# A fused attention, expert and MLP kernel: input conversion and transposition, token tiles and weight conversion in more stages, and one more GpSimd DRAIN

## Chip, core and metric

The kernel runs on one core of a Trainium2 chip. The metric is the device time of one execution in microseconds. Engines are named as in the profile: PE (TensorE matmul), PEld (its weight loads), DVE (VectorE), ACT (ScalarE), POOL (GpSimd), SP (SyncE, which here only issues DMAs). A "q" behind an engine's name is its sequencer.

## The reference

```python
scores_l = scale * np.matmul(q, k.transpose(0, 1, 3, 2))     # local window of 16, plus block summaries
a = softmax(concat(masked scores_l, scores_s + log(32)))
x = a @ concat(v, v_sum)                                     # (2, 8, 768, 64) -> 1536 tokens x 512
logits = x @ w_gate; noise_scale = log1p(exp(x @ w_noise))
top2 of (logits + noise_scale * noise), softmax weights
out[token] = sum over its 2 experts: weight * (relu(x @ w1[e]) @ w2[e])     # 8 experts, 512 -> 1024 -> 512
h = out @ w_in; g = relu(h) ** 2; result = g @ w_out         # 512 -> 2048 -> 512
```

All data are float32. Matrix products of the last two stages are made of three passes of a rounded float32 type: a high part times a high part, and two products with a low part, so each operand exists as a high tile (xh, wh, hh) and a low tile (xl, wl, hl).

## The kernel before

**Attention**, to about 140 us in the trace, is untouched by the change. It scatters every token's row into a table xg with one region for each expert.

**Units.** From then on the kernel is a loop over units g. Units 0 to 63 are eight experts (e = g // 8) of eight units each (f = g % 8); units 64 to 111 are three chunks of 512 tokens with 16 units each. In unit g PE does `h_unit(g)`, 12 matmuls into a PSUM tile ph, and then the second half of the unit before, `y_unit(g - 1)` or `o_part`, 12 matmuls into acc. Each engine and SP's queue run in the order in which the code emits their instructions; there is no scheduler in this part. The order within a unit is: the matmuls and what follows ph (ACT writes hh, DVE hl, at lines 771 and 772 for experts, 765 to 769 for chunks), `y_store` at an expert's first unit, the split of the weights three units ahead (`w_split`: ACT wh at line 186, DVE wl at line 190, then SP's load of the weights wr six units ahead into the buffer just freed), the steps of `plan`, the next expert's input, the table steps, and last `conv`.

**Next expert's input.** `x_load(e)` has SP read the region of expert e from xg into xin. `x_turn` first calls `x_flip` (DVE transposes of 32 x 32 blocks, xin to xtt, line 217), and then ACT writes xh (line 227). `x_rest` writes xl, on POOL when the source is xtt. The four column chunks c go to units f = 3, 4, 5, 6; under expert 0 two each to units 5 and 6. `x_load(e + 2)` comes behind chunk 3, `x_load(1)` at unit 2. `fill(e)`, at units 1, 4, 7 and so on to 19, has POOL write zeros into a part of xg by an indirect DMA; each x_load waits for all fills ahead of it in the program, and each fill for the x_loads ahead of it.

**Weight conversion.** The last stage's weights come as eight-byte words. `conv` turns 32 pieces (units in CG: 1, 3, 5, 7, 9, 12, ...): SP loads cr, `conv_bits` does four ACT instructions (lines 823 to 826) into the tiles c0, c1 and c2, `conv_end` two DVE instructions one unit later, and `conv_store` one unit after that stores c0 to w2f with a DMA on SP's queue. The pool cv gives each of these tiles two buffers, so the first ACT instruction of a piece (line 823) waits until the store of the piece before the last has landed.

**Token tiles.** Tiles t of 128 tokens pass through `gather` (POOL indirect DMAs from yg), `mix` (ACT line 1154, DVE line 1155, and a store to x2d on SP), `swap` (SP reads x2d back in another order) and `spread` (DVE transpose at line 1176 into z4, ACT xh at line 1182, DVE xl at line 1183). GT, GB, G0 and G1 say in which unit each step stands. Chunk 1 is first read in unit 80, chunk 2 in unit 96.

**End.** Four indirect DMAs on POOL write the last output tiles; a loop that runs zero times here follows (line 1308), then the closing barrier with a DRAIN of each engine (line 1363).

Of the kernel before, what the change touches and what calls it, by code (L numbers as in the profile page):

```python
# [22 lines left out]
DM = H * D  # L23
E = 8
# [109 lines left out]
def moe_pipeline_kernel(ctx: ExitStack, tc: tile.TileContext, qT, kT, vW, mk, idm, wg, noise, w1, w2, out):  # L134
# [85 lines left out]
    def x_turn(e, c, src=None):  # L220
        if c == 0:
            xh_t[e] = xp.tile([128, 4, 512], F32R, name="xh")
            xl_t[e] = xp.tile([128, 4, 512], F32R, name="xl")
        if src is None:
            x_flip(e, c)
            src = xt_t[e][:, c, 0:CAPS[e]]
        nc.scalar.activation(out=xh_t[e][:, c, 0:CAPS[e]], in_=src, func=AF.Copy)  # L227

    def x_rest(e, c, src=None):
# [585 lines left out]
    def conv_bits(i):  # L815
# [279 lines left out]
    def overflow():  # L1095
        n = nc.values_load(trips[0:1, 0:1], min_val=0, max_val=nck)
        with tc.For_i(0, n, 1):
# [11 lines left out]
            xt = yb.tile([128, DM], F32, name="x2")  # L1109
# [42 lines left out]
    def blend(ys, gates):  # L1152
        x2 = yb.tile([128, DM], F32, name="x2")
# [31 lines left out]
    def late_tokens():  # L1185
        n = nc.values_load(trips[0:1, 1:2], min_val=0, max_val=NT)
        with tc.For_i(0, n, 1):
# [9 lines left out]
            xt = yb.tile([128, DM], F32, name="x2")  # L1197
# [169 lines left out]
```

## Time and profile before

| | |
|---|---|
| median of 3 runs | 724.45 us (719.29 to 729.62) |
| profiled execution | 722.66 us, its span 720.9 us |
| mean granted clock of TensorE over the span | 0.956 |
| busy in the span: PE, DVE, ACT, POOL | 652.8, 431.9, 364.3, 134.6 us |
| expert and chunk stages on PE | 139.6 to 707.5 us |

A profiled execution is one run, and lies 1.8 us under the median. PE's busy time counts pipelined matmuls whose ends are modelled: two rows that follow each other without a pause overlap.

### The profile page before, as it was taken

To read this page: it belongs to the slowest core of one execution; us is meant where nothing else is said; L and a number is where in the kernel's file an instruction comes from. 1 tells how busy PE (TensorE), PEld (TensorE's weight loads), DVE (VectorE), ACT (ScalarE), POOL (GpSimd) and SP (SyncE) were. 2 spreads that over 40 slices of the span, in tenths; PEclk is the share of its full clock that TensorE was granted. 3 is DMA by queue.
4 is the path that set the end of the run, shared out by engine and by line. 5 is a ranking of instruction groups with operands and counts; after the bars stand their busy time and mean duration, and the time that the engine had idled before them with its cause. 6 is when DMAs were issued, how large, how long until landed. Compare 5 with 4: busy or idle time off the path is not lost.

```text
span 720.9 us, 11094 instructions
## 1 busy us (share of the span) xinstructions
PE 652.8 (91%) x3928; PEld 574.0 (80%) x3928; DVE 431.9 (60%) x952; ACT 364.3 (51%) x708; POOL 134.6 (19%) x199
## 2 busy tenths in 40 slices
PE   5787776998998899999999979999999999999992
PEld 4666554797998799899999878788888888888881
DVE  5757554585767676756575656666665565644530
ACT  3676351255563564667466656654454455434330
POOL 3000434313130111335113400310024100300002
PEclk9999776799999999999999999999999999999997
DMA  8877326279988777788878787865437555432101
GB/s 229 198 186 177 138 89 209 83 258 316 292 320 268 262 224 264 200 276 247 248 223 301 253 257 249 250 201 156 135 106 241 147 160 132 145 116 90 59 1 61
DMA packets 75739, 139.97 MB, mean 194 GB/s; under 512 B 9042, under 2 KB 44162, under 8 KB 74895
## 3 DMA queue, kind: packets, MB, share of 16 engines
q1 hardware_dynamic: 69566, 116.95, 55.4%
q0 software_dynamic: 6112, 22.25, 8.3%
q8 instruction: 33, 0.54, 0.3%
q14 instruction: 28, 0.22, 0.1%
HBM read 103.27 MB, written 34.88 MB: 192 GB/s over the span
## 4 chain that ended last, share of the span: by engine, by line
PE 31%; DMA 24%; issue 15%; ACT 11%; DVE 10%; SPq 4%; another core or an unknown queue 2%; POOL 1%; DVEq 0%; ACTq 0%; POOLq 0%
DMA w2f<-c 6%; DMA vB<-in_vW_dram 5%; PE ph L750 4%; PE ph L748 4%; PE ph L749 4%; DVE wl L190 4%; PE acc L748 4%; PE acc L749 4%; PE acc L750 4%; DMA wr<-in_w_dram 3%; ACT wh L186 3%; DMA yg<-ys 3%; DMA vB<-vm 2%; DMA xg<-z,tb_gi 2%
## 5 line engine op out<-in xcount | busy, mean ns | idle before, releaser
L750 PE MATMUL ph<-xl,wh 128*128 128x512 f32 (+8 forms) x448 | 163.0, 364 | 1.8 <-POOL xl L233 1.8
L748 PE MATMUL ph<-xh,wh 128*128 128x512 f32 (+8 forms) x448 | 162.9, 364 | 0.4 <-ACT xh L1182 0.4
L749 PE MATMUL ph<-xh,wl 128*128 128x512 f32 (+8 forms) x448 | 162.5, 363 | 0.0
L190 DVE TENSOR_TENSOR wl<-wr,wh 128x1024 fp32r<-128x1024 f32 x112 | 137.1, 1224 | 28.6 <-ACT wh L186 25.8
L186 ACT ACTIVATE wh<-wr 128x1024 fp32r<-128x1024 f32 x112 | 117.5, 1049 | 4.5 <-DMA wr<-in_w_dram 4.5
L748 PE MATMUL acc<-hh,wh 128*128 128x416 f32 (+7 forms) x256 | 89.4, 349 | 11.1 <-ACT hh L771 11.0
L750 PE MATMUL acc<-hl,wh 128*128 128x416 f32 (+7 forms) x256 | 90.2, 352 | 3.8 <-DVE hl L772 3.7
L750 PEld LDWEIGHTS ph<-xl,wh 128*128 128x128 f32 x448 | 84.2, 188 | 11.2 <-POOL xl L233 2.8
L748 PEld LDWEIGHTS ph<-xh,wh 128*128 128x128 f32 x448 | 84.3, 188 | 8.5 <-ACT xh L1182 0.8
L749 PEld LDWEIGHTS ph<-xh,wl 128*128 128x128 f32 x448 | 84.2, 188 | 7.6
L749 PE MATMUL acc<-hh,wl 128*128 128x416 f32 (+7 forms) x256 | 88.3, 345 | 0.0
L772 DVE SCALAR_TENSOR_TENSOR hl<-ph,hh 128x416 fp32r<-128x416 f32 (+7 forms) x64 | 36.5, 570 | 71.1 <-ACT hh L771 71.1
L748 PE MATMUL acc<-wh,hh 128*128 128x512 f32 x192 | 74.8, 389 | 0.6 <-DVE ys L797 0.6
L749 PE MATMUL acc<-wh,hl 128*128 128x512 f32 x192 | 74.8, 390 | 0.0
L750 PE MATMUL acc<-wl,hh 128*128 128x512 f32 x192 | 74.7, 389 | 0.0
L765 ACT ACTIVATE hr<-ph 128x512 f32<-128x512 f32 x48 | 28.7, 598 | 81.5 <-PE ph L750 81.5
L766 DVE SCALAR_TENSOR_TENSOR hg<-ph,hr 128x512 f32<-128x512 f32 x48 | 33.1, 691 | 60.5 <-ACT hr L765 56.9
L748 PEld LDWEIGHTS acc<-hh,wh 128*128 128x128 f32 x256 | 48.6, 190 | 14.5 <-ACT hh L771 14.3
L233 POOL TENSOR_TENSOR xl<-xtt,xh 128x424 fp32r<-128x424 f32 (+6 forms) x28 | 31.7, 1135 | 134.0 <-ACT xh L227 134.0
L750 PEld LDWEIGHTS acc<-hl,wh 128*128 128x128 f32 x256 | 48.7, 190 | 9.6 <-DVE hl L772 9.2
L769 DVE TENSOR_TENSOR hl<-hg,hh 128x512 fp32r<-128x512 f32 x48 | 33.3, 693 | 33.5 <-ACT hh L768 32.8
L768 ACT ACTIVATE hh<-hg 128x512 fp32r<-128x512 f32 x48 | 30.3, 632 | 39.2 <-DVE hg L766 39.2
(246 smaller groups left out, 934.7 us busy)
## 6 DMA issues: line engine op xcount, KB each, us to landing
wr<-in_w_dram SPq DMA_DIRECT2D x64, 512.0 KB
wr<-w2f SPq DMA_DIRECT2D x48, 512.0 KB
cr<-in_w_dram SPq DMA_DIRECT2D x32, 512.0 KB
w2f<-c SPq DMA_DIRECT2D x32, 256.0 KB
vB<-in_vW_dram SPq DMA_DIRECT2D x8, 576.0 KB
xin<-xg SPq DMA_DIRECT2D x20, 208.0 KB
kB<-in_kT_dram SPq DMA_DIRECT2D x16, 200.0 KB
yg<-ys SPq DMA_DIRECT2D x16, 192.0 KB
```

The costliest lines, as they stand in the source:

```text
L186: nc.scalar.activation(out=hi_t[i], in_=raw_t[i], func=AF.Copy)
L190: nc.vector.tensor_tensor(out=lo_t[i], in0=raw_t.pop(i), in1=hi_t[i].bitcast(F32), op=OP.subtract)
L233: eng.tensor_tensor(out=xl_t[e][:, c, 0:n], in0=src, in1=xh_t[e][:, c, 0:n].bitcast(F32), op=OP.subtract)
L748: nc.tensor.matmul(out=o, lhsT=wh, rhs=xh, start=first, stop=False)
L749: nc.tensor.matmul(out=o, lhsT=wl, rhs=xh, start=False, stop=False)
L750: nc.tensor.matmul(out=o, lhsT=wh, rhs=xl, start=False, stop=last)
L765: nc.scalar.activation(out=r[:, 0:n], in_=p[:, 0:n], func=AF.Relu)
L766: nc.vector.scalar_tensor_tensor(out=gg[:, 0:n], in0=p[:, 0:n], scalar=0.0, in1=r[:, 0:n], op0=OP.max, op1=OP.mult)
L768: nc.scalar.activation(out=hh[:, 0:n], in_=gg[:, 0:n], func=AF.Copy)
L769: nc.vector.tensor_tensor(out=hl[:, 0:n], in0=gg[:, 0:n], in1=hh[:, 0:n].bitcast(F32), op=OP.subtract)
L772: nc.vector.scalar_tensor_tensor(out=hl[:, 0:n], in0=p[:, 0:n], scalar=0.0, in1=hh[:, 0:n].bitcast(F32), op0=OP.max, op1=OP.subtract)
```

## The change

It edits the order of the unit loop in five places and moves one kind of work.

- The transposition of the next expert's input stands one unit ahead of xh, and xl one unit behind it: `x_flip` at f = 2 to 5, `x_turn` at 3 to 6, `x_rest` at 4 to 7. Under expert 0 the flips are in units 4 and 5. `x_load(e + 2)` follows the flip of chunk 3, so it stands one unit earlier.
- `x_rest` runs on DVE for all experts; POOL has no work on xl left.
- `conv_bits` is cut into `conv_high` and `conv_low`, two ACT instructions each, in two units that follow each other; `conv_end` and `conv_store` come one unit later. c0 has three buffers.
- `spread` is cut into `flip` (the DVE transpose) and `spread` (xh and xl) one unit later, and the tile x2 has four buffers. The first four tiles are gathered at units 49, 50, 52, 53 (before 51, 53, 55, 56), and their spread stands at units 58, 59, 61, 62 (before 57, 59, 61, 62). For the chunks 1 and 2 the flip stands where the spread stood and the spread one unit later, so the last spread of a chunk is in units 79 and 95 (before 78 and 94).
- A GpSimd DRAIN without any wait stands at unit 106. The instruction before it on POOL is the last output DMA of chunk 1, in unit 96, so POOL's queue reaches it there.

```diff
-XF = 3
+XF = 2
+X0 = {4: (0, 1), 5: (2, 3)}
-GB = 51
+GB = 49
+CB = (3, 2, 2)
-GT = (0, 2, 4, 5)
-G0 = (0, 3, 4, 6)
-G1 = (0, 3, 4, 6)
+GT = (0, 1, 3, 4)
+G0 = (0, 4, 5, 8, 9)
+G1 = (0, 3, 4, 6, 7)
...
     def x_rest(e, c, src=None):
-        eng = nc.gpsimd if src is None else nc.vector
         n = CAPS[e]
         src = xt_t[e][:, c, 0:n] if src is None else src
-        eng.tensor_tensor(out=xl_t[e][:, c, 0:n], in0=src, in1=xh_t[e][:, c, 0:n].bitcast(F32), op=OP.subtract)
+        nc.vector.tensor_tensor(out=xl_t[e][:, c, 0:n], in0=src, in1=xh_t[e][:, c, 0:n].bitcast(F32), op=OP.subtract)
...
-        w, r = c_t[i] = [cv.tile([128, 512], d, name=f"c{j}") for j, d in enumerate((F32, I32))]
-        sg = cv.tile([128, 512], BF, name="c2")
+        w, r, sg = c_t[i] = [cv.tile([128, 512], d, name=f"c{j}", bufs=CB[j]) for j, d in enumerate((F32, I32, BF))]
         nc.scalar.activation(out=w, in_=hi, func=AF.Copy, scale=2.0 ** -112)
         nc.scalar.activation(out=sg, in_=hi, func=AF.Sign)
+    def conv_low(i):
...
-        x2 = yb.tile([128, DM], F32, name="x2")
+        x2 = yb.tile([128, DM], F32, name="x2", bufs=4)
...
+    def flip(t):
+        xs, xt = x2_t.pop(t), z4[:, (t % 4) * DM:(t % 4 + 1) * DM]
+        nc.vector.transpose(out=xt.rearrange("p (n j) -> p n j", j=32), in_=xs.rearrange("p (n j) -> p n j", j=32))
     def spread(t):
         ci, i = divmod(t, 4)
-        xs, xt = x2_t.pop(t), z4[:, (t % 4) * DM:(t % 4 + 1) * DM]
-        nc.vector.transpose(out=xt.rearrange("p (n j) -> p n j", j=32), in_=xs.rearrange("p (n j) -> p n j", j=32))
+        xt = z4[:, (t % 4) * DM:(t % 4 + 1) * DM]
...
-        if g in CG:
-            conv_bits(CG.index(g))
-        if g - 1 in CG:
-            conv_end(CG.index(g - 1))
-        if g - 2 in CG:
-            conv_store(CG.index(g - 2))
+        for d, fn in enumerate((conv_high, conv_low, conv_end, conv_store)):
+            if g - d in CG:
+                fn(CG.index(g - d))
...
+        if g == n1 + n2 - 6:
+            nc.gpsimd.drain()
...
-        for c in ({5: (0, 1), 6: (2, 3)}.get(f, ()) if e == 0 else range(f - XF, f - XF + 1)):
-            if e + 1 == E or not 0 <= c < 4:
-                continue
-            x_turn(e + 1, c)
-            x_rest(e + 1, c)
-            if c == 3 and e + 2 < E:
-                x_load(e + 2)
+        if e + 1 < E:
+            for d, fn in enumerate((x_flip, x_turn, x_rest)):
+                for c in X0.get(f - d, ()) if e == 0 else range(f - d - XF, f - d - XF + 1):
+                    if 0 <= c < 4:
+                        fn(e + 1, c)
+                        if d == 0 and c == 3 and e + 2 < E:
+                            x_load(e + 2)
```

DVE before, units 4 and 5 of expert 0 (hl and wl open a unit, c0 is `conv_end`, tb_ are table steps, xtt is the flip):

```order
L772 SCALAR_TENSOR_TENSOR hl_2204<-ph_2190,hh_2203 128x416
L190 TENSOR_TENSOR wl_2220<-wr_2032,wh_2219 128x1024
L946 CAST trips_1902<-tb_pre_2063 1x1
L866 TENSOR_TENSOR tb_d1_2228<-tb_begin_2067,tb_cnt_2038 128x8
L866 TENSOR_TENSOR tb_base_2227<-tb_d1_2228,tb_pre_2063 128x8
L866 TENSOR_TENSOR tb_d2_2229<-row8_84,tb_cnt_2038 128x8
L832 TENSOR_SCALAR c0_2182<-c0_2182 128x512
L833 ISA c0_2182<-c0_2182,c1_2183 128x1024
L772 SCALAR_TENSOR_TENSOR hl_2251<-ph_2237,hh_2250 128x416
L190 TENSOR_TENSOR wl_2267<-wr_2112,wh_2266 128x1024
L217 STREAM_TRANSPOSE xtt_2274<-xin_2124 128x448 x2
```

And in the changed kernel, the same two units:

```order
L772 SCALAR_TENSOR_TENSOR hl_2201<-ph_2187,hh_2200 128x416
L192 TENSOR_TENSOR wl_2217<-wr_2032,wh_2216 128x1024
L219 STREAM_TRANSPOSE xtt_2222<-xin_2122 128x448 x2
L949 CAST trips_1902<-tb_pre_2063 1x1
L869 TENSOR_TENSOR tb_d1_2228<-tb_begin_2067,tb_cnt_2038 128x8
L869 TENSOR_TENSOR tb_base_2227<-tb_d1_2228,tb_pre_2063 128x8
L869 TENSOR_TENSOR tb_d2_2229<-row8_84,tb_cnt_2038 128x8
L772 SCALAR_TENSOR_TENSOR hl_2252<-ph_2238,hh_2251 128x416
L192 TENSOR_TENSOR wl_2268<-wr_2110,wh_2267 128x1024
L219 STREAM_TRANSPOSE xtt_2222<-xin_2122 128x448 x2
```

The first two flips stand ahead of hl and wl of unit 5, where they stood behind them.

POOL before, from the last set-up DMA to the tables of the early tokens (tb_gi marks the fills, x2 two that follow each other):

```order
L927 DMA xg_74<-z4_1908,tb_ri_2053 16384x512
L854 DMA xg_74<-z4_1908,tb_gi_1907 4096x2048 x2
L233 TENSOR_TENSOR xl_2273<-xtt_2274,xh_2272 128x424 x4
L854 DMA xg_74<-z4_1908,tb_gi_1907 4096x2048 x2
L233 TENSOR_TENSOR xl_2574<-xtt_2575,xh_2573 128x410 x3
L854 DMA xg_74<-z4_1908,tb_gi_1907 4096x2048
L233 TENSOR_TENSOR xl_2574<-xtt_2575,xh_2573 128x410
L854 DMA xg_74<-z4_1908,tb_gi_1907 4096x2048
L233 TENSOR_TENSOR xl_2967<-xtt_2968,xh_2966 128x400
L854 DMA xg_74<-z4_1908,tb_gi_1907 4096x2048
```

And in the changed kernel:

```order
L930 DMA xg_74<-z4_1908,tb_ri_2053 16384x512
L857 DMA xg_74<-z4_1908,tb_gi_1907 4096x2048 x7
L1019 IOTA tb_ids_3122 128x12
L1020 MEMSET tb_rec_3121 128x96
L1021 COPY tb_rec_3121<-tb_ids_3122 128x12
```

All seven fills stand in a row, with no xl between them.

DVE before, units 94 and 95, the last ones ahead of chunk 2 (hg, hl and wl are each unit's own work; units 78 and 79 ahead of chunk 1 read alike):

```order
L766 SCALAR_TENSOR_TENSOR hg_6510<-ph_6494,hr_6509 128x512
L769 TENSOR_TENSOR hl_6508<-hg_6510,hh_6507 128x512
L190 TENSOR_TENSOR wl_6528<-wr_6403,wh_6527 128x1024
L1176 STREAM_TRANSPOSE z4_1908<-x2_6405 128x512
L1183 TENSOR_TENSOR xl_6266<-z4_1908,xh_6265 128x4x128
L766 SCALAR_TENSOR_TENSOR hg_6552<-ph_6536,hr_6551 128x512
L769 TENSOR_TENSOR hl_6550<-hg_6552,hh_6549 128x512
L190 TENSOR_TENSOR wl_6570<-wr_6446,wh_6569 128x1024
```

And in the changed kernel:

```order
L766 SCALAR_TENSOR_TENSOR hg_6510<-ph_6494,hr_6509 128x512
L769 TENSOR_TENSOR hl_6508<-hg_6510,hh_6507 128x512
L192 TENSOR_TENSOR wl_6528<-wr_6401,wh_6527 128x1024
L1178 STREAM_TRANSPOSE z4_1908<-x2_6405 128x512
L766 SCALAR_TENSOR_TENSOR hg_6550<-ph_6534,hr_6549 128x512
L769 TENSOR_TENSOR hl_6548<-hg_6550,hh_6547 128x512
L192 TENSOR_TENSOR wl_6568<-wr_6446,wh_6567 128x1024
L1189 TENSOR_TENSOR xl_6313<-z4_1908,xh_6312 128x4x128
```

The last tile's xl stands behind hl and wl of unit 95, directly ahead of the work of unit 96.

## Rows read from the trace of the kernel before

**Rows 1.** Windows of 60 us: PE, PEld, DVE, ACT, POOL busy (instructions), clock, DMA share.

```profile
140.00:200.00 60.00, 57.08 (x297) 54.73 (x296) 43.35 (x100) 34.30 (x53) 13.79 (x31) 1.00 0.87 275
200.00:260.00 60.00, 55.10 (x283) 51.93 (x283) 40.02 (x74) 31.87 (x52) 12.32 (x14) 1.00 0.79 262
260.00:320.00 60.00, 58.20 (x328) 56.50 (x327) 41.67 (x82) 36.03 (x58) 13.01 (x16) 1.00 0.84 259
320.00:380.00 60.00, 59.38 (x330) 57.69 (x330) 37.92 (x70) 37.10 (x60) 16.01 (x21) 1.00 0.81 231
380.00:440.00 60.00, 53.85 (x296) 51.08 (x294) 37.72 (x61) 35.77 (x57) 14.70 (x12) 0.97 0.84 271
440.00:500.00 60.00, 58.71 (x261) 48.35 (x262) 39.46 (x57) 35.31 (x53) 8.73 (x9) 1.00 0.69 212
```

**Rows 2.** Waits of PE: engine, line, awaited: us, times, longest.

```profile
PE acc L748 <- ACT hh L771: 11.0, 8, 2.6
...
PE acc L750 <- DVE hl L772: 3.7, 7, 1.3
...
PE ph L750 <- POOL xl L233: 1.8, 3, 0.7
```

**Rows 3.** Waits of all engines, the rows on ACT.

```profile
ACT xh L227 <- DVE xtt L217: 50.7, 25, 4.1
...
ACT xh L1182 <- DVE z L1176: 27.7, 12, 4.0
ACT c L823 <- DMA w2f<-c: 26.8, 9, 6.9
```

**Rows 4.** Chain of work, 205 to 240: start, us, piece.

```profile
208.79 1.43 POOL xl L233
210.37 8.21 DMA xg<-z,tb_gi
...
220.54 4.91 DMA w2f<-c
```

**Rows 5.** Waits of SP's queue.

```profile
SPq L211 <- DMA xg<-z,tb_gi: 12.9, 2, 6.8
```

**Rows 6.** Tile xl: duration min/median/max in ns, first and last start.

```profile
L233 POOL TENSOR_TENSOR xl<-xtt,xh x28: 1009/1081/1548, 169.1 to 402.7; 128x424 fp32r<-128x424 f32 x4, 128x410 fp32r<-128x410 f32 x4, 128x400 fp32r<-128x400 f32 x4, 128x394 fp32r<-128x394 f32 x4
...
L1183 DVE TENSOR_TENSOR xl<-z,xh x12: 691/693/693, 414.9 to 615.0; 128x512 fp32r<-128x512 f32 x12
```

**Rows 7.** Timeline of DVE, units 4 and 5.

```profile
159.59 1.23 DVE L190 TENSOR_TENSOR wl<-wr,wh 128x1024 fp32r<-128x1024 f32 x1 [0.36 <-ACT wh L186]
...
167.50 1.17 DVE L217 STREAM_TRANSPOSE xtt<-xin 128x448 f32<-128x448 f32 x2 [2.17 <-DMA xin<-xg]
```

**Rows 8.** Timeline of PE, unit 6, where it reads unit 5's hl.

```profile
167.30 0.35 PE L750 MATMUL acc<-hl,wh 128*128 128x416 f32 x1
167.49 0.35 PE L748 MATMUL acc<-hh,wh 128*128 128x416 f32 x1
```

**Rows 9.** Timeline of units 78 to 80.

```profile
527.29 0.63 ACT L1182 ACTIVATE xh<-z 128x512 fp32r<-128x512 f32 x1 [1.91 <-DVE z L1176]
...
527.96 0.69 DVE L1183 TENSOR_TENSOR xl<-z,xh 128x512 fp32r<-128x512 f32 x1 [0.70 <-ACT xh L1182]
...
529.82 1.05 ACT L186 ACTIVATE wh<-wr 128x1024 fp32r<-128x1024 f32 x1
...
530.34 0.39 PE L748 MATMUL ph<-xh,wh 128*128 128x512 f32 x1
...
530.90 1.23 DVE L190 TENSOR_TENSOR wl<-wr,wh 128x1024 fp32r<-128x1024 f32 x1 [0.26 <-ACT wh L186]
```

**Rows 10.** Line 1363, the kernel's end: duration min/median/max in ns, first and last start.

```profile
L1363 POOLq DRAIN  x3: 40/103/6611, 713.4 to 720.6; - x3
...
L1363 PEldq DRAIN  x2: 8/8/8, 713.8 to 720.4; - x2
```

**Rows 11.** Windows of 4 us around the one fall of the clock.

```profile
429.00:433.00 4.00, 3.19 (x11) 3.20 (x12) 1.88 (x3) 1.37 (x3) 0.00 (x0) 0.57 0.89 340
```

More of the change, by code (lines that the diff above doesn't have):

```diff
@@ L223, in x_turn, with x_rest @@
             xl_t[e] = xp.tile([128, 4, 512], F32R, name="xl")
[L224 to L229, printed above, removed]
-        eng = nc.gpsimd if src is None else nc.vector
         n = CAPS[e]
         src = xt_t[e][:, c, 0:n] if src is None else src
-        eng.tensor_tensor(out=xl_t[e][:, c, 0:n], in0=src, in1=xh_t[e][:, c, 0:n].bitcast(F32), op=OP.subtract)
+        nc.scalar.activation(out=xh_t[e][:, c, 0:n], in_=src, func=AF.Copy)
+    def x_rest(e, c, src=None):
+        n = CAPS[e]
+        src = xt_t[e][:, c, 0:n] if src is None else src
+        nc.vector.tensor_tensor(out=xl_t[e][:, c, 0:n], in0=src, in1=xh_t[e][:, c, 0:n].bitcast(F32), op=OP.subtract)
     def attention(ctx):
@@ L813, in conv_load, with conv_high @@
                           in_=w2[f].bitcast(I32)[:, s * 1024:(s + 1) * 1024])
-    def conv_bits(i):
-        lo, hi = c_raw[i][:, :, 0].bitcast(U32), c_raw[i][:, :, 1].bitcast(F32)
-        w, r = c_t[i] = [cv.tile([128, 512], d, name=f"c{j}") for j, d in enumerate((F32, I32))]
-        sg = cv.tile([128, 512], BF, name="c2")
-        half = r.bitcast(U16).rearrange("p (c b) -> p c b", b=2)
+    def conv_high(i):
+        hi = c_raw[i][:, :, 1].bitcast(F32)
+        w, r, sg = c_t[i] = [cv.tile([128, 512], d, name=f"c{j}", bufs=CB[j]) for j, d in enumerate((F32, I32, BF))]
         nc.scalar.activation(out=w, in_=hi, func=AF.Copy, scale=2.0 ** -112)
         nc.scalar.activation(out=sg, in_=hi, func=AF.Sign)
+    def conv_low(i):
+        lo = c_raw[i][:, :, 0].bitcast(U32)
+        w, r, sg = c_t[i]
+        half = r.bitcast(U16).rearrange("p (c b) -> p c b", b=2)
         nc.scalar.activation(out=half[:, :, 0], in_=lo, func=AF.Copy, scale=2.0 ** -29)
@@ L828, in conv_end @@
     def conv_end(i):
-        w, r = c_t[i]
+        w, r, sg = c_t[i]
         t = w.bitcast(I32)
@@ L1108, in overflow @@
                 nc.tensor.transpose(p[:, c, :], xq[:, c * 128:(c + 1) * 128], ident)
-            xt = yb.tile([128, DM], F32, name="x2")
+            xt = yb.tile([128, DM], F32, name="x2", bufs=4)
             nc.vector.tensor_copy(out=xt, in_=p.rearrange("p a b -> p (a b)"))
@@ L1196, in late_tokens @@
             p = turn(ys[0])
-            xt = yb.tile([128, DM], F32, name="x2")
+            xt = yb.tile([128, DM], F32, name="x2", bufs=4)
             nc.vector.tensor_copy(out=xt, in_=p.rearrange("p a b -> p (a b)"))
@@ L1264, in moe_pipeline_kernel @@
         g = GB + GT[t] if t < 4 else n1 + GA + 2 * (t - 4) if t < 8 else n1 + FC2 + GA + 2 * (t - 8)
-        for d, fn in zip(G0 if t < 4 else G1, (gather, mix, swap, spread)):
+        for d, fn in zip(G0 if t < 4 else G1, (gather, mix, swap, flip, spread)):
             plan.setdefault(g + d, []).append((fn, t))
     for g in range(n1 + n2 + 1):
+        if g == n1 + n2 - 6:
+            nc.gpsimd.drain()
         if g == n1 + n2 - 2:
```

## The prediction

> **What bounds the kernel now.** I first looked at windows of 60 us over the expert and early chunk stages, to see where PE is not busy. PE is idle 2.92, 4.90, 1.80, 0.62, 6.15 and 1.29 us in the six windows from 140 to 500 us, 17.68 us in all [rows 1]; behind 500 us it runs without a pause until its work ends at 707.5 us. So PE is the bound, and apart from the tail only these pauses can be won. A pause is a little longer than it shows: a matmul row is 0.35 us long and the next starts 0.19 us after it, so 0.16 us of each pause hides under the modelled end [rows 8]. The waits of PE, read next, name 18 pauses behind hh, hl and xl [rows 2], which makes 2.9 us more. In one stretch the granted clock also falls: a window of 4 us at 429 us has a mean of 0.57 [rows 11], which is the lower of the two levels (1.2 of 2.4 GHz) for most of it, behind a window in which PE mostly waited. That costs 0.43 x 4 = 1.7 us. The budget of the stages is 17.7 + 2.9 + 1.7 = 22.3 us.
>
> Who is late? Mostly ACT: PE waits 11.0 us for hh, 3.7 us for hl and 1.8 us for xl [rows 2]. ACT itself waits in its queue, ahead of the next hh, on three things [rows 3]: 50.7 us in 25 waits for a flip that DVE does in the same unit, 27.7 us in 12 waits for the DVE transpose of a token tile, and 26.8 us in 9 waits for a store of the weight conversion. The chain of work shows how the longest of the last kind comes about [rows 4]: POOL's xl at 208.79 us, behind it a fill of 8.21 us, which SP awaits before x_load(3), and behind that x_load, on the same queue, the store to w2f, issued at 220.54 us and landed 4.91 us later. SP lost 12.9 us in two such waits for a fill [rows 5].
>
> The tail is the second thing. Behind the last output POOL's DRAIN alone takes 6.61 us, from 713.4 us, while PE's stands there at 713.8 us and takes 8 ns [rows 10].
>
> **The change part by part.** *Weight conversion.* Cut in two, its four ACT instructions no longer stand as one block between two hh. The third buffer gives a store one piece more, two to three units of 24 x 0.19 = 4.5 us [rows 8] less the one unit by which it now comes later, so about 4.5 us net. That covers most of the nine waits, whose mean is 26.8 / 9 = 3.0 us and whose longest is 6.9 us [rows 3]. The instructions themselves are as many as before.
>
> *Fills and x_load.* Without xl on POOL a fill waits only for DMAs. x_load(3) moves from unit 14 to 13, ahead of the fill in that unit, so it waits only for the fill of unit 10: the second of SP's two waits [rows 5] goes, and the store behind it is issued about 6 us earlier. x_load(2) moves from unit 6 to 5, only one unit behind a fill, and may wait there; behind it on SP stand weights that wait for wl anyway, so I cost it at nothing, and at up to one unit's slip of a load if that cover is gone.
>
> *Flip ahead of xh.* ACT's 50.7 us go: each flip is done a unit earlier. DVE has no more flips than before.
>
> *xl on DVE.* POOL takes 1.08 us at the median, DVE needs 0.69 us for 512 columns [rows 6], so about 0.57 us for the 374 to 424 here; 28 of them are 16 us, over 56 units. DVE is busy 38 to 43 of 60 us [rows 1], about 3.1 us of a unit's 4.5, and the new work adds 0.57 us in every second unit. It waits for an xh of the unit before, which is done. I cost it at nothing outside the first expert; the cover is DVE's 1.4 us of idle time in a unit.
>
> *The first flips.* Here the change adds a wait. DVE reached the flips at unit 5 and still had to wait until 167.50 us for xin; they last 1.17 us together [rows 7]. In unit 4 it reaches them once wl ends at 159.59 + 1.23 = 160.82 us, and is held for 6.7 us with hl and wl of unit 5 queued behind. The flips end at 168.67, four small table steps and hl (0.6 us each, an estimate for the steps from their count) at about 169.8 us. PE wants that hl at 167.30 us [rows 8]: 2.5 us. DVE is then late for the xl of chunks 2 and 3, which stand in unit 7 behind wl; that costs between 0 and 1.7 us, and I take 1.0, nearer to its middle since nothing in the trace has this order. Against that stand the 2.92 us of this window [rows 1], which the two conversion edits take away. So 3.5 us stay here where 2.92 were.
>
> *Token tiles.* For the first four tiles the flip comes three units behind the swap instead of two, and the mix four behind the gather, which takes out most of the 27.7 us of ACT's waits [rows 3] and with them the window of 380 to 440 us. SP still waits for each x2d store one unit behind it, so not all of it goes. For chunks 1 and 2 the last spread comes one unit ahead of its first use. In unit 79 ACT's wh ends at 529.82 + 1.05 = 530.87, xh takes 0.63 more, to 531.50 us; DVE's wl ends at 530.90 + 1.23 = 532.13, xl takes 0.69, to 532.82 us. PE begins unit 80 at 530.34 us with xh, and needs xl two matmuls (0.45 us) later, at 530.79 us [rows 9]. So PE waits 2.0 us, once for each of two chunks: 4.0 us that were not there.
>
> *DRAIN.* It costs POOL nothing where it stands: on POOL's queue only the four output DMAs of chunk 2 follow it, at the kernel's end. What it may save is the 6.61 us at the end. The next thing that is late there is PE's DRAIN at 713.8 us, so the gain is at most 713.4 + 6.6 - 713.8 = 6.2 us [rows 10]. The trace has one long DRAIN, behind all the indirect DMAs, and two of 0.04 and 0.10 us right behind it. If its length is work that piles up with every indirect DMA, or a cost of the first one, the early DRAIN takes nearly all of it; if it belongs to the last four DMAs, none. I take the first as the likelier of two, because the DRAINs right behind it show that one is short on a queue that has just been drained, and keep both ends, 0 and 6.2. The Trainium skill (PSUM — Partial Sum Buffer, Engine vs sequencer instructions) says that a drain waits until the engine is fully idle. By that rule a DRAIN at a time when POOL is idle would take nothing off a later one that follows four new DMAs, and the sum would be the one without the 6.2 us, which is the first rival below.
>
> *Sum.* The windows keep 3.5, 0.5, 0.6, 0.2, 1.5 and 0.8 us of their 17.68 us, 7.1 in all: the last five are estimates, a tenth to a third of what each window loses where the awaited thing moves by a unit, and more in the last, where a wait for the transposes of y_store stays. That is -10.6 us, with the clock -1.7, and with 10 pauses fewer of 0.16 us -1.6: -13.9. The spreads give +4.0, the DRAIN -6.2. Together -16.1 us. From the profiled execution's own 722.66 us that leaves 706.6 us; from the median of 724.45 us it would be 708.3. I say 707.
>
> **The rivals.** *The long DRAIN stays at the end.* For it speaks that four indirect DMAs follow the early one, and that the trace shows no short DRAIN behind such DMAs; against it that 6.6 us is long for four. Time: 722.66 - 9.9 = 712.8 us.
>
> *The transfers, not the order, are late.* The store takes 4.91 us from issue and a fill 8.21 us [rows 4], and DMA engines are 79 to 87% busy in four of these windows [rows 1]. Steps that are one unit apart, as x_load(2) behind its fill and swap behind mix, would still wait on SP, and half of the 13.9 us would stay. Time: 722.66 - 7.0 + 4.0 = 719.7 us, or 713.5 if the DRAIN moves. Against it speaks that the longest wait came from the order of POOL's and SP's queues.
>
> *VectorE becomes the bound, and the kernel is slower.* Its 1.4 us of idle time in a unit are waits for hh and wh of the same unit. Should the 0.57 us not fit into them, each of the 28 lengthens a unit: 16 us, and the old pauses stay. With the spreads and the first flips (+4.6) this gives 722.66 + 20.6 = 743.3 us, or 737.1 with a shorter tail. It decides from the point where DVE's work in units f = 4 and 5 (hl, wl, flip, xl, a conversion's end and tables) passes 4.5 us again and again. Against it speaks that hl has almost a unit of slack: PE reads it only behind the next unit's first half.
>
> **How the numbers follow.** Forecast 0.42; DRAIN stays 0.33; transfers late 0.19; VectorE 0.06. The forecast's own spread is about 4 us either way, its lower end with every pause gone at 722.66 - 22.3 + 4.0 - 6.2 = 698.2 us. A range of 699 to 721 us takes in the first three cases and leaves out little of them, and all of the fourth. Two per cent, about what a measurement of this kernel can tell from no change, lies at 710.0 us below and 738.9 us above: faster holds four fifths of the forecast (0.34), a quarter of the second case (0.08) and a little of the third (0.03), in all 0.45; slower, most of the fourth, 0.05; within it 0.50.
>
> **What the profile would show.** If I am right, ACT's waits for xtt and for w2f nearly vanish, SP waits for a fill once and not twice, and PE has a pause of about 2.5 us near unit 6 for hl of line 772 and one of about 2 us at each of units 80 and 96, for xh and then for xl. POOL has a long DRAIN near 630 us and a short one at the end. The clock stays at its upper level from unit 1 to the end of PE's work. I am wrong if PE still waits for hh in the window of 200 to 260 us, if the DRAIN at the end keeps its length, if waits for hl grow in the units that have xl, or if the pauses at units 80 and 96 bring the clock down, which would cost more than they do themselves.

## The result, and the profile after

The changed kernel takes 697.08 us (median of 4 runs, 692.52 to 699.84) against 723.41 us (4 runs): a ratio of 0.961, 95% interval 0.956 to 0.966. That is 26.3 us faster, where 16 were forecast, and 2 us below the low end of the range. Ratios are taken from the chip's fast state alone; the profiled execution of one kernel below, b_drain, was in the slow one, and no length is read from it.

The profiled execution took 692.52 us, the shortest of its four and 4.6 us under their median, with a span of 690.5 us. Set beside the span of before (720.9 us), three stretches make up the difference of 30.4 us. PE's first matmul of unit 0 starts at 136.67 us and not 139.39: 2.7 us in the attention, whose code is the same. From there to the start of PE's last matmul, in the following called **PE's stages**, it takes 545.73 us and not 567.75: 22.0 us. The rest, to the end of the span, takes 8.1 us and not 13.8: 5.7 us. These are the first and the last matmul of that stretch, before and after:

```profile
139.39 0.35 PE L748 MATMUL ph<-xh,wh 128*128 128x416 f32 x1
...
707.13 0.39 PE L750 MATMUL acc<-wl,hh 128*128 128x512 f32 x1
```

```profile
136.67 0.35 PE L748 MATMUL ph<-xh,wh 128*128 128x416 f32 x1
...
682.40 0.39 PE L750 MATMUL acc<-wl,hh 128*128 128x512 f32 x1
```

Windows of 60 us of the changed kernel, which answer to [rows 1], with two more (columns: window, its length, PE, PEld, DVE, ACT, POOL busy, granted clock, DMA share, GB/s):

```profile
140.00:200.00 60.00, 58.38 (x309) 56.94 (x308) 45.73 (x109) 36.20 (x56) 5.71 (x7) 1.00 0.94 305
200.00:260.00 60.00, 60.00 (x335) 59.65 (x334) 48.40 (x100) 37.31 (x58) 3.39 (x7) 1.00 0.96 293
260.00:320.00 60.00, 60.00 (x336) 60.00 (x335) 43.08 (x80) 39.24 (x63) 14.44 (x23) 1.00 0.88 260
320.00:380.00 60.00, 60.00 (x344) 60.00 (x344) 45.16 (x83) 40.59 (x65) 8.98 (x8) 1.00 0.90 285
380.00:440.00 60.00, 60.00 (x322) 56.01 (x321) 43.59 (x72) 38.44 (x60) 6.78 (x6) 1.00 0.85 272
440.00:500.00 60.00, 60.00 (x266) 49.69 (x265) 37.88 (x49) 31.75 (x46) 1.99 (x3) 1.00 0.55 162
500.00:560.00 60.00, 58.50 (x257) 47.78 (x256) 32.39 (x40) 27.24 (x39) 13.90 (x16) 1.00 0.51 162
560.00:620.00 60.00, 58.50 (x257) 47.84 (x256) 33.85 (x43) 26.85 (x39) 5.68 (x8) 1.00 0.44 132
```

PE shows no idle time at all from 200 to 500 us. What is left is 1.62 us in the first window and 1.5 us in each of the last two. The waits name them, and those of ACT and SP [rows 2, 3, 5] (engine, line, awaited: us, times, longest):

```profile
ACT xh L228 <- DVE xtt L219: 3.3, 1, 3.3
ACT c L821 <- DMA w2f<-c: 2.4, 3, 1.7
...
PE ph L748 <- ACT xh L1188: 1.8, 2, 0.9
...
PE acc L750 <- DVE hl L772: 1.3, 1, 1.3
...
PE ph L750 <- DVE xl L1189: 1.2, 2, 0.6
...
PE ph L750 <- DVE xl L233: 0.3, 1, 0.3
```

ACT's 50.7 us of waits for flips are down to 3.3 and its 26.8 us for stores to 2.4, and its waits for the token tiles' transposes have no row any more. PE waits once for hl, near unit 6, once briefly for xl in the unit after next, and twice for xh and then xl, at units 80 and 96. SP still waits twice for a fill, 9.1 us where it was 12.9:

```profile
SPq L213 <- DMA xg<-z,tb_gi: 9.1, 2, 6.8
```

The DRAINs of POOL's queue, the new one at line 1272 and the closing ones at line 1368, which answer to [rows 10] (operation and count: shortest, median, longest in ns, first and last start):

```profile
L1272 POOLq DRAIN  x1: 8600/8600/8600, 602.3 to 602.3; - x1
...
L1368 POOLq DRAIN  x3: 52/103/393, 689.3 to 690.2; - x3
```

The closing DRAIN fell from 6.61 to 0.39 us. The early one starts at 602.3 us (near 630 was forecast), while POOL still issues the last output of chunk 1; that DMA is off POOL at 604.6 us, and 6.3 us of the DRAIN follow it. Nobody waits for it.

PE's timeline at the pause near unit 6 shows what a pause costs beside its idle time (start, us, instruction, in brackets the idle time before it and what ended it):

```profile
164.22 0.35 PE L748 MATMUL acc<-hh,wh 128*128 128x416 f32 x1
164.41 0.34 PE L749 MATMUL acc<-hh,wl 128*128 128x416 f32 x1
166.09 0.46 PE L750 MATMUL acc<-hl,wh 128*128 128x416 f32 x1 [1.34 <-DVE hl L772]
166.39 0.35 PE L748 MATMUL acc<-hh,wh 128*128 128x416 f32 x1
```

Undisturbed rows start 0.19 us apart. Here the start-to-start time is 1.68 us, so 1.49 us are lost where 1.34 show as idle; and the first row after the pause is longer, 0.46 us, so that the next starts 0.30 us behind it, 0.11 more than usual. A pause costs its idle time and about 0.26 us (0.15 + 0.11).

### The profile page after: what moved, and what is told of

Same layout as the page of the kernel before. It is cut to its first block, busy times and chain, and to the rows that moved or that the text cites. A ratio compares the mean times of both kernels' runs of the same rounds, so it can differ in the third digit from the quotient of the medians.

```text
span 690.5 us, 11121 instructions
## 1 busy us (share of the span) xinstructions
PE 640.0 (93%) x3928; PEld 572.5 (83%) x3928; DVE 440.9 (64%) x980; ACT 365.7 (53%) x708; POOL 100.0 (14%) x171
## 5 line engine op out<-in xcount | busy, mean ns | idle before, releaser
L750 PE MATMUL acc<-hl,wh 128*128 128x416 f32 (+7 forms) x256 | 87.8, 343 | 1.3 <-DVE hl L772 1.3
L748 PE MATMUL acc<-hh,wh 128*128 128x416 f32 (+7 forms) x256 | 87.7, 342 | 0.0
L771 ACT ACTIVATE hh<-ph 128x416 fp32r<-128x416 f32 (+7 forms) x64 | 32.1, 502 | 80.2 <-PE ph L750 74.8
L354 ACT ACTIVATE es<-z,bi 128x120 f32<-128x120 f32 x96 | 36.6, 383 | 25.9 <-DVE bi L347 25.9
```

What stands on the lines that cost most here:

```text
L354: nc.scalar.activation(out=e_t[s][:, i, h], in_=z, func=AF.Exp, bias=bi, scale=-1.0, accum_out=sums[:, b * QT + t0 + i, c:c + 1])
L748: nc.tensor.matmul(out=o, lhsT=wh, rhs=xh, start=first, stop=False)
L750: nc.tensor.matmul(out=o, lhsT=wh, rhs=xl, start=False, stop=last)
L771: nc.scalar.activation(out=hh[:, 0:n], in_=p[:, 0:n], func=AF.Relu)
```

## The experiments

The kernel before took 707.8 to 728.3 us on the chips of these runs; on two of them unit 0 begins at 121 to 125 us, on the others at 137 to 146. So kernels are compared by their ratio to the kernel before on the same chip, and by PE's stages in the profiled execution: their length, how much of it PE shows as idle with the longest pause, and for how long the granted clock was at the lower of its two levels (twice what the mean granted clock of the stages lacks to 1.00, times their length):

| kernel | ratio to before (95%) | PE's stages, us | idle in them, longest pause, us | at the lower clock, us |
|---|---|---|---|---|
| before | 1 | 567.75 | 17.7, 2.64 | 3.4 |
| changed | 0.961 (0.956 to 0.966) | 545.73 | 4.6, 1.34 | 0 |
| a_no_drain | 0.969 (0.965 to 0.974) | 548.21 | 6.4, 1.45 | 0 |
| b_drain | 0.993 (0.990 to 0.996) | | | |
| a_drain36 | one run | 548.04 | 5.7, 1.57 | 0 |
| a_conv_whole | 0.986 (0.980 to 0.993) | 566.99 | 19.6, 4.73 | 13.7 |
| a_xl_pool | 0.966 (0.959 to 0.973) | 559.25 | 14.4, 4.80 | 6.8 |
| a_flip_late | 0.972 (0.964 to 0.979) | 556.49 | 9.2, 1.55 | 0 |
| a_tiles_old | 0.964 (0.956 to 0.972) | 549.03 | 6.3, 3.43 | 3.4 |
| b_conv | 0.985 (0.977 to 0.992) | 559.92 | 11.0, 3.74 | 10.2 |
| b_c0 | 0.984 (0.977 to 0.992) | 560.80 | 11.5, 2.78 | 13.7 |
| b_xl | 1.009 (1.005 to 1.013) | 576.91 | 23.4, 5.24 | 6.8 |
| b_stage | 0.994 (0.990 to 0.998) | 567.20 | 16.3, 5.12 | 20.5 |
| b_stage_xl | 0.989 (0.983 to 0.996) | 567.19 | 18.6, 4.55 | 17.1 |
| a_g1 | 0.956 (0.948 to 0.965) | 542.87 | 2.4, 1.77 | 0 |
| a_g1_x0 | 0.955 (0.948 to 0.961) | 544.57 | 4.1, 3.07 | 0 |
| a_g1_x1 | 0.949 (0.944 to 0.955) | 541.50 | 1.4, 0.81 | 0 |

Names that begin with a_ are edits of the changed kernel, with b_ of the kernel before. a_no_drain and a_drain36 have the changed kernel's order in all of PE's stages; their 548.2 and 548.0 us beside 545.7 show that single executions scatter by some 2.5 us, and differences of that size are read from the pauses themselves. Where the clock falls the scatter is wider: the four runs of a_xl_pool lie between 683.92 and 691.85 us, and the profiled one is the slowest. So what an edit costs is given by the ratios too.

**The DRAIN: a_no_drain, b_drain, a_drain36.**

```diff
-        if g == n1 + n2 - 6:          # a_no_drain; b_drain adds these two lines to before
-            nc.gpsimd.drain()
+        if g == 36:                   # a_drain36
+            nc.gpsimd.drain()
```

> The changed kernel without its one new GpSimd DRAIN. If the early DRAIN is what shortens the end, the closing DRAIN on POOL is again 6 to 7 us long (0.39 us with the early one) and the time rises by 5.5 to 6.5 us, to about 703 us; PE's work between unit 0 and its last matmul keeps its length within 0.3 us. If the end became short for another reason (no xl work on POOL, fills that land earlier), the closing DRAIN stays under 1 us and the time stays at 697.

> The kernel before with the new DRAIN alone. If the DRAIN's saving is its own: the early DRAIN is 6 to 9 us long, the closing one about 0.4 us, the time falls by 5.5 to 6.5 us (ratio 0.991 to 0.993), and no pause of PE changes. If the saving needs the rest of the change, ratio 1.00 and a closing DRAIN of about 6.6 us.

> The changed kernel with its DRAIN moved from unit 106 to unit 36, where 44 of the 80 indirect DMAs are behind it on POOL and 36 follow, where it was 76 and 4. Two theories. Work that piles up with every indirect DMA (6.61 us for 80 is 0.083 us each): the early DRAIN takes about 3.6 us and the closing one about 3.0 us, and the time rises by 2.6 us. A cost of the first long DRAIN in a program: the early one takes about 6.3 us, the closing one 0.4 us, and the time does not change. If only the DMAs since the last output wait matter, the closing one is 6.6 us.

Closing DRAINs of a_no_drain, and the early and closing DRAINs of a_drain36:

```profile
L1366 POOLq DRAIN  x3: 40/103/6611, 691.1 to 698.3; - x3
```

```profile
L1272 POOLq DRAIN  x1: 5512/5512/5512, 288.7 to 288.7; - x1
...
L1368 POOLq DRAIN  x3: 52/103/3578, 694.4 to 698.5; - x3
```

Without the early DRAIN the closing one has its 6.61 us again, and the ratio rises by 0.008, some 6 us; PE's stages are 2.5 us longer where 0.3 was expected, which is the scatter named above. On the kernel before, the DRAIN alone gives a ratio of 0.993, some 5 us. From the start of PE's last matmul to the end of the span it takes 13.8 us before and 13.5 in a_no_drain, 8.1 us in the changed kernel and 10.9 in a_drain36. So the saving is its own. Its length piles up with the indirect DMAs since the last DRAIN: 6.61 us behind 80, 3.58 us behind 43 (in a_drain36, where 37 stand ahead of the early one by their order on POOL, not 44 as expected), 0.39 us behind 4. The early one of a_drain36 ends at 294.2 us, 3.1 us behind the end of the 37th. With the 6.3 us behind 76 of the changed kernel's early one that is 0.082 to 0.084 us for each DMA, and 0.098 behind only 4. A cost of the first DRAIN alone would have left 0.4 us behind 43.

**One edit taken out: a_conv_whole, a_xl_pool, a_flip_late, a_tiles_old.**

```diff
-CB = (3, 2, 2)                        # a_conv_whole
+CB = (2, 2, 2)
-        for d, fn in enumerate((conv_high, conv_low, conv_end, conv_store)):
+        for d, fns in enumerate(((conv_high, conv_low), (conv_end,), (conv_store,))):
...
-        nc.vector.tensor_tensor(      # a_xl_pool, in x_rest where the source is xtt
+        nc.gpsimd.tensor_tensor(
...
-XF = 2                                # a_flip_late: x_flip, x_turn, x_rest of c in one unit
+XF = 3                                # (units 5 and 6 under expert 0)
...
-GB = 49                               # a_tiles_old
-GT = (0, 1, 3, 4)
-G0 = (0, 4, 5, 8, 9)
-G1 = (0, 3, 4, 6, 7)
+GB = 51
+GT = (0, 2, 4, 5)
+G0 = (0, 3, 4, 6, 6)
+G1 = (0, 3, 4, 6, 6)
```

> The changed kernel with the weight conversion as it was: four ACT instructions in one unit, two buffers of c0, the store one unit earlier. Theory: the store to w2f is the largest cause of the pauses of before (9 waits of ACT, 26.8 us), so ACT waits for w2f again, PE pauses of 8 us or more in all for hh and hl come back between 200 and 440 us, and the time rises by 8 to 12 us. Rival: what made the store late was SP's queue held behind fills and xl on POOL, both of which stay mended here; then ACT's waits for w2f stay under 8 us, PE's pauses under 2 us, and the time within 2 us.

> The changed kernel with xl of the experts' inputs on POOL again, in the places where it now stands. Theory (conversion is the cause, POOL only adds to it): fills are again held behind xl, SP waits for them up to 13 us, PE loses at most 2 us, mostly for xl itself in the first expert. Rival (POOL's queue is the cause): pauses for hh of 4 to 7 us in all come back between 200 and 260 us.

> The changed kernel with flip, xh and xl of the next expert's input in one unit again (units 5 and 6 for the first expert, f = 3 to 6 else; xl stays on DVE). Theory: ACT waits for flips again for some 50 us, but this slack is mostly covered; PE loses 2 to 5 us, of it 2 to 3.5 in units 6 and 7 in place of the 1.9 us there now. Rival: the wait for the flips was the main cause of the pauses, and 8 us or more come back.

> The changed kernel with the token tiles in the units of before (gather at 51, 53, 55, 56, flip and spread in one unit, four buffers of x2 kept). The pauses at units 80 and 96 (4.2 us) vanish. Theory: the window of 380 to 440 us loses 3 to 6 us again, which about balances, so the time is within 2 us of the changed kernel. Rival: those pauses came from the conversion, and the kernel is 3 to 4 us faster than the changed one.

*a_conv_whole* loses 21.3 us of PE's stages, nearly the whole gain; by the ratios it is 0.025, some 18 us. Both are more than the 8 to 12 us of the theory. Its waits, then PE's timeline at its longest pause, and the windows behind it:

```profile
ACT c L821 <- DMA w2f<-c: 33.7, 9, 9.3
...
PE acc L748 <- ACT hh L771: 9.3, 2, 4.7
```

```profile
218.84 0.35 PE L750 MATMUL ph<-xl,wh 128*128 128x410 f32 x1
223.91 0.71 PE L748 MATMUL acc<-hh,wh 128*128 128x410 f32 x1 [4.73 <-ACT hh L771]
224.42 0.55 PE L749 MATMUL acc<-hh,wl 128*128 128x410 f32 x1
```

```profile
223.90:227.90 4.00, 3.98 (x12) 3.79 (x13) 3.60 (x6) 3.96 (x7) 0.00 (x0) 0.50 0.72 257
227.90:229.00 1.10, 1.10 (x5) 1.07 (x4) 1.10 (x3) 1.10 (x3) 0.00 (x0) 0.50 0.85 335
```

ACT waits for w2f again, 33.7 us where it was 26.8, and PE loses its time in fewer and longer pauses. Behind the 4.73 us of idle time the granted clock is 0.50, the lower level, for 5.1 us, and rows stand 0.34 us apart: 2.5 us more for this pause. The clock falls at two more places, at pauses of 3.11 and 4.53 us. In all it is at the lower level for 13.7 us, and up to half of that, 6.8 of the 21.3 us, is the clock's. In the kernel before, whose longest wait is 2.6 us, it fell once, in a window of 4 us [rows 2, 11].

*a_xl_pool* loses 13.5 us in its profiled execution; by the ratios it is 0.005, some 4 us, within the intervals, so the size of this loss is not settled. The places are not those of the rival: the pauses stand at unit 6, for hl, and at unit 16, for xl. DVE and POOL at unit 4:

```profile
152.34 0.17 DVE L870 TENSOR_TENSOR tb_base<-tb_d,tb_pre 128x8 f32<-128x8 f32 x1
152.43 2.42 DVE L870 TENSOR_TENSOR tb_d<-row,tb_cnt 128x8 f32<-128x8 f32 x1
154.76 0.58 DVE L773 SCALAR_TENSOR_TENSOR hl<-ph,hh 128x416 fp32r<-128x416 f32 x1
```

```profile
152.68 2.13 POOL L234 TENSOR_TENSOR xl<-xtt,xh 128x424 fp32r<-128x424 f32 x2
```

A table step of eight columns lasts 2.42 us, where its like lasts 0.17, as long as POOL's two xl run beside it, and hl stands behind it: 2.3 us of a pause of 4.4. The pair b_stage and b_stage_xl below, which differ in the engine of xl alone, shows the same step at the same place, first with xl on POOL and then with xl on DVE:

```profile
154.02 2.42 DVE L870 TENSOR_TENSOR tb_d<-row,tb_cnt 128x8 f32<-128x8 f32 x1
```

```profile
152.75 0.16 DVE L869 TENSOR_TENSOR tb_d<-row,tb_cnt 128x8 f32<-128x8 f32 x1
```

With all xl on DVE (the changed kernel, b_xl, b_stage_xl) no step is stretched in this way. In the kernel before seven DVE instructions are, each while POOL runs an xl; they are 4.7 us longer than the median of their like, together. The pause at unit 16 comes from POOL's queue, PE first and then POOL:

```profile
206.55 0.71 PE L751 MATMUL ph<-xl,wh 128*128 128x410 f32 x1 [4.80 <-POOL xl L234]
```

```profile
204.47 0.95 POOL L858 DMA_INDIRECT xg<-z,tb_gi  x1 [14.74 <-DMA xin<-xg]
205.44 2.06 POOL L234 TENSOR_TENSOR xl<-xtt,xh 128x410 fp32r<-128x410 f32 x2
```

The fill waits 14.7 us for an x_load, and xl stands behind the fill.

*a_flip_late* loses 10.8 us (by the ratios 0.011, some 8 us), in 14 pauses of up to 1.55 us between 158 and 384 us, 6.2 us of idle time and the rest hidden beside it; ACT waits for flips again:

```profile
ACT xh L228 <- DVE xtt L219: 53.0, 28, 3.5
```

That is over the 2 to 5 us of the theory and bears the rival out. *a_tiles_old* loses 3.3 us, by the ratios 0.003: the 4.2 us at units 80 and 96 go, ACT waits for transposes again, and one pause of 3.4 us for xh stands at unit 64, with 3.4 us at the lower clock behind it. That is near the balance that the theory expected:

```profile
ACT xh L1188 <- DVE z L1178: 28.0, 12, 4.5
...
PE ph L748 <- ACT xh L1188: 3.4, 1, 3.4
```

**One edit alone: b_conv, b_c0, b_xl, b_stage, b_stage_xl.**

```diff
-    [cv.tile([128, 512], d, name=f"c{j}") for j, d in enumerate((F32, I32))]             # b_c0
+    [cv.tile([128, 512], d, name=f"c{j}", bufs=3 - j) for j, d in enumerate((F32, I32))]
...
-        eng = nc.gpsimd if src is None else nc.vector                                    # b_xl
+        eng = nc.vector
```

b_conv has conv_high, conv_low, CB and conv of the diff above, b_stage the three stages of the flips (XF, X0 and the loop over x_flip, x_turn, x_rest), b_stage_xl these and the line of b_xl; these three keep the four buffers of x2.

> The kernel before with the new weight conversion alone (cut in two, store one unit later, three buffers of c0; flips, xl on POOL, tiles and DRAIN as before, four buffers of x2). Putting the old conversion back into the changed kernel cost 17 to 21 us. If the conversion acts alone, this kernel wins 12 us or more of PE's stages, ACT's waits for w2f fall from 26.8 to under 5 us, and the ratio is about 0.98. If it only acts together with a free POOL and SP queue, ACT still waits for w2f for 8 us or more and the gain is under 6 us (ratio over 0.99).

> The kernel before with a third buffer of c0 and nothing else: conversion uncut, stores where they were. If the buffer is what ends ACT's waits for w2f (26.8 us in 9), they fall under 5 us and PE's stages shorten by 8 us or so, as with the whole new conversion. If the cut in two matters as much (ACT's four instructions in one block ahead of hh), under half of that is won.

> The kernel before with xl on VectorE alone (flip, xh and xl in one unit, conversion, tiles, x_load as before, no DRAIN). If the chain from xl on POOL over the fill, SP's x_load(3) and the store to w2f makes the pauses of 200 to 260 us (6.9 us with their hidden parts), SP's longest wait for a fill shrinks to 1 us or less there, ACT's longest wait for w2f falls from 6.9 to under 4 us, and PE wins 4 to 6 us in that window, little elsewhere: ratio about 0.99. If VectorE's new 16 us are what counts, waits for hl grow and the ratio is 1.00 or above. If the two buffers of c0 decide, ACT's waits for w2f stay near 27 us.

> The kernel before with flip, xh and xl of the next expert's input in three units that follow each other (as changed, x_load one unit earlier with them), xl on POOL, conversion, tiles and end as before. Theory (staging is what lets the other edits pay): ACT's 50.7 us of waits for flips nearly vanish, PE's stages shorten by 4 to 8 us. Rival (it only moves slack, and the first flips hold hl): under 2 us either way.

> As b_stage, with xl on VectorE. Theory: with the staging xl on VectorE no longer waits for xh of its own unit, so it does not lengthen the unit as it did alone (+9 us), and this kernel is faster than b_stage by 2 us or more. Rival: VectorE's 16 us of new work cost 5 us or more here too, and this kernel is slower than b_stage; then the changed kernel's gain from xl must come through the conversion.

*b_c0* wins 6.9 us of PE's stages and *b_conv* 7.8 (by the ratios 0.016 and 0.015, 11 us each): the third buffer does it, and what the cut in two adds is within the scatter (no run has it alone). b_conv lies between its two cases, with 4.4 us of ACT's waits for w2f left; in b_c0 none is left. Both spend 10 us and more at the lower clock, the kernel before 3.4. SP's waits for fills are as long as before, 13.8 us in 3:

```profile
SPq L211 <- DMA xg<-z,tb_gi: 13.8, 3, 6.8
```

So with a third buffer a store may land as late as those waits make it, and ACT does not wait for it. *b_xl* says the same from the other side, and is slower than before, by 9.2 us in PE's stages and 0.009 in the ratio (some 6 us):

```profile
PE acc L748 <- ACT hh L771: 13.3, 11, 5.2
...
PE acc L750 <- DVE hl L772: 7.7, 11, 1.3
...
ACT c L823 <- DMA w2f<-c: 23.3, 8, 9.8
```

PE's waits for VectorE's hl grew, as one of its expectations had it, and the waits for w2f stayed near those of before, as another had it. With POOL free of xl, x_load(3) no longer waits for a fill: SP has one such wait left, of 6.8 us, and reaches this x_load at 216.2 us and issues it at 216.3. Yet ACT's longest wait for w2f grew to 9.8 us, because behind the x_load eight stores of yg and their waits stand ahead of the store to w2f on SP's queue (222 to 232 us). The chain of waits had named the link that came last; when it went, the next one held as long.

*b_stage* gains nothing in PE's stages of its profiled execution (567.20 us), and with xl on VectorE added (*b_stage_xl*) it is the same (567.19). By the ratios they are faster than before by 0.6% (0.2 to 1.0) and 1.1% (0.5 to 1.7). What the staging changed is the kind of pause: b_stage is idle for 16.3 us where the kernel before was for 17.7, but in 9 pauses and not in 22, the longest 5.12 us for hl at unit 6 and 3.37 us for xl at unit 16. And the clock fell at three places, these two and two pauses of 1.14 and 1.34 us in unit 61:

```profile
157.00:164.00 7.00, 5.94 (x17) 5.68 (x18) 6.93 (x13) 3.60 (x6) 3.13 (x2) 0.51 0.89 281
208.00:216.00 8.00, 6.73 (x22) 6.31 (x23) 3.41 (x10) 3.87 (x6) 3.13 (x4) 0.57 0.62 253
413.00:420.00 7.00, 6.39 (x21) 6.39 (x22) 2.87 (x5) 3.79 (x6) 0.00 (x0) 0.51 0.82 273
```

That is 20.5 us at the lower level, up to 10.2 us lost, where the kernel before lost up to 1.7. So this execution does not show that staging is worth nothing; it shows that staging alone left fewer and longer pauses, and that the clock fell in three places. Staged, xl on VectorE costs nothing that the runs show (the ratios of the two differ by 0.005, within their intervals); unstaged it costs 9.2 us.

**The pauses that the change brought: a_g1, a_g1_x0, a_g1_x1.**

```diff
-G1 = (0, 3, 4, 6, 7)                                   # all three
+G1 = (0, 3, 4, 6, 6)
-X0 = {4: (0, 1), 5: (2, 3)}                            # a_g1_x1; a_g1_x0 has {7: (0, 1, 2, 3)} for xl
+X0 = ({5: (0, 1), 6: (2, 3)}, {6: (0, 1), 7: (2, 3)}, {6: (0, 1), 7: (2, 3)})   # flip, xh, xl
...
-                for c in X0.get(f - d, ()) if e == 0 else ...
+                for c in X0[d].get(f, ()) if e == 0 else ...
```

> The changed kernel with flip and spread of the tiles of chunks 1 and 2 in one unit again, as before, the first four tiles as changed. The pauses ahead of and in units 80 and 96 (2.1 us each, 1.05 for xh and 0.78 for xl with their hidden parts) vanish, nothing else changes in PE's stages, and the time falls by 4.2 us (ratio against the kernel before lower by 0.006). If ACT, which then waits for each flip in the same unit, makes hh late, half or more of the 4.2 us comes back as pauses for hh between units 64 and 96.

> As the kernel with flip and spread together, and besides the first expert's flips in units 5 and 6 again, xh one unit behind them in 6 and 7, all four xl in unit 7. The pause for hl at unit 6 (1.5 us, and 0.4 for xl at unit 7) falls to 0.5 us or less, since DVE reaches the flips after hl and wl of unit 5 and xin has nearly landed: 1.5 us faster than with the first edit alone. If four xl behind hl and wl are too much for unit 7 (0.6 + 1.2 + 4 x 0.6 = 4.2 of 4.5 us), PE waits 1 to 3 us for xl or hl in unit 8, and nothing is won.

> As the kernel with flip and spread of the tiles together (which lost nothing and won the two pauses), and the first expert's flips in units 5 and 6, xh and xl one unit behind in units 6 and 7, two chunks each. The run with all four xl in unit 7 moved the wait from hl (1.9 us) to xl (3.2 us at unit 8). With two xl in unit 6, both pauses should stay under 1 us in all, and PE's stages last 541 us or a little less, 1.5 us under those of the first edit alone. If the time at which xin lands decides, DVE is held at unit 5 and a pause of 1 us or more for hl or xl stays in units 6 to 8.

In a_g1 the pauses at units 80 and 96 are gone and none came for hh there, so the 4.2 us are won; PE's stages are 2.9 us shorter, as other pauses of this execution were longer (1.77 us for hl at unit 6). In a_g1_x0 the wait went from hl to xl (3.07 us at unit 8) and nothing was won, as its rival said. a_g1_x1 has both right; its window at the first flips and the two with units 80 and 96:

```profile
140.00:200.00 60.00, 59.62 (x316) 58.40 (x315) 45.67 (x107) 36.48 (x56) 7.57 (x28) 1.00 0.85 284
...
500.00:560.00 60.00, 60.00 (x266) 49.71 (x265) 33.80 (x42) 27.36 (x39) 13.89 (x16) 1.00 0.52 164
560.00:620.00 60.00, 60.00 (x266) 49.67 (x266) 35.00 (x44) 28.02 (x41) 5.68 (x8) 1.00 0.47 137
```

It has the lowest ratio of all, 0.949 (0.944 to 0.955) against 0.961 (0.956 to 0.966) of the changed kernel; the intervals of a_g1 and a_g1_x0 overlap with its own.

## Why the prediction was wrong

The sign and the mechanisms of the likeliest case were right; the size was not, and the time fell below the range. The term that failed is the sum over PE's pauses: forecast -13.9 + 4.0 = -9.9 us, measured -22.0 us in PE's stages.

- **The price of a pause.** I took 0.16 us beside its idle time; it is about 0.26, by the rows above. Behind a pause for hh it is more, as in the kernel before, PE and then DVE:

```profile
228.43 0.45 PE L748 MATMUL acc<-hh,wh 128*128 128x410 f32 x1 [2.27 <-ACT hh L771]
...
229.04 0.45 PE L750 MATMUL acc<-hl,wh 128*128 128x410 f32 x1
```

```profile
228.40 0.58 DVE L772 SCALAR_TENSOR_TENSOR hl<-ph,hh 128x410 fp32r<-128x410 f32 x1 [4.51 <-ACT hh L771]
```

The row with hl shows no idle time, yet it waited: hl ends at 228.98 us, and the row stands 0.61 us behind the first one, where two undisturbed steps are 0.37. Added up start to start against undisturbed rows, the stages of before lose about 28 us: 21.2 in the 22 steps with visible idle time (17.7 of it the idle time itself), and some 7 in about 50 others that are 0.1 us or more too long, the stretch of lower clock among them. My budget was 22.3. This is about 5.7 us of the miss.
- **What stays.** I kept 3.6 us in the windows from 200 to 500 us, as a tenth to two thirds of what each lost. No idle time stayed there, nor the hidden parts of those pauses: some 5 us.
- **The first flips.** Forecast 3.5 us, measured 2.1 with hidden parts (1.34 us idle for hl, 0.28 for xl): 1.4 us of the miss.
- **Spreads one unit ahead of use.** Forecast 2.0 us at each of units 80 and 96; measured 2.1, for xh and then xl, and the clock did not fall. Right. With these four terms the 12.1 us are accounted for, but for some tenths. By a_no_drain and a_drain36, which have the same order, the stages are 19.6 us shorter and the miss is nearer to 10 us; the rest lies within the scatter of single executions.
- **The conversion.** Nine waits, 26.8 us, down to 2.4: right, and by the buffer, as argued. That without it the changed kernel's stages are only 0.8 us shorter than those of before I did not see: the edits don't add. In PE's stages the conversion alone wins 7.8 us, the staging nothing, and xl loses 9.2; taken out, they cost 21.3, 10.8 and 13.5. By the ratios it is 0.015, 0.006 and -0.009 alone, and 0.025, 0.011 and 0.005 taken out, the last within its interval. A part of this is the clock, which I followed only through the changed kernel: PE's stages are at the lower level for 7 to 20 us in each of the kernels with the conversion, the staging or xl alone, and for none of the time in the changed kernel. For the rest it fits that ACT has all of these late pieces in one queue and PE waits for what is late last, so that one edit alone uncovers the next cause; no run separates the two.
- **Fills and x_load.** I said that one of SP's two waits would go. Two waits stayed (9.1 us in all), and no pause of PE with them. The step from [rows 4] to a cause was wrong, as b_xl and b_c0 show.
- **xl on VectorE, costed at nothing.** Right where it is staged, wrong alone. The rival of a VectorE that becomes the bound comes nearest in b_xl, at 9 us and not 20. What I left out on the other side is that xl on POOL held VectorE's own work, 4.7 us in the kernel before.
- **The DRAIN.** Forecast at most 6.2 us, measured 5.7. Its length grows with every indirect DMA since the last one, the first of my two readings; that it is a cost of the first DRAIN is out by a_drain36. The Trainium skill (PSUM — Partial Sum Buffer, Engine vs sequencer instructions) says that a drain waits until the engine is fully idle. What the first rival made of it, that a DRAIN on an idle queue takes nothing off the last one, did not hold: 6.61 us became 0.39.
- **The clock** is 1.00 in all windows from 140 to 620 us, as said.
- **A misreading without weight.** DMA engines are 79 to 87% busy in five of the six windows of [rows 1], not in four. The second rival has that much more for it, and fell all the same: no idle time stayed from 200 to 500 us.

The median moved by 26.3 us and the profiled execution by 30.1; 2.7 of the latter lie ahead of unit 0, where the code is the same.

## What to carry to other kernels

Count the price of a bound engine's pauses start to start against an undisturbed stretch, not by idle time. Where several producers share one in-order queue, edits that each remove a wait need not add: test them taken out of the whole as well as alone, and look at the granted clock of each run before its length is put down to the edit. Believe the last link of a chain of waits only if removing it moves the end. A DRAIN on GpSimd's queue in an idle stretch takes work off the closing one when many indirect DMAs stand ahead of it.

## What the runs showed of the hardware

- POOL's DRAIN took 0.08 to 0.10 us for each indirect DMA since the last DRAIN on its queue: 6.61, 3.58 and 0.39 us behind 80, 43 and 4.
- While POOL ran two xl (2.13 us), a VectorE step of eight columns took 2.42 us instead of 0.17. The Trainium skill (SBUF — State Buffer, Terms) says that DVE and GpSimd have a port pair in common whose lock is held for a whole instruction while the other blocks. These rows agree, with VectorE as the one that is held; which step takes the lock no run here shows.
- A PE pause of 4.73 us was followed by 5.1 us at a granted clock of 0.50 (a_conv_whole). Behind one of 3.07 us in a_g1_x0 the clock stayed at 1.00. Fewer pauses did not mean less time at the lower level: b_stage has 9 pauses and 20.5 us of it, the kernel before 22 and 3.4.
